# The order of loads at the start of a fused attention and two-layer kernel: one key load to another queue, one weight load earlier, a first weight piece cut smaller

## The chip, the cores and the metric

The kernel runs on one core of one Trainium2 chip. The metric is device time in microseconds (us) of one execution. Where this text gives times inside an execution, they are read from one profiled execution and counted from its first instruction. Engines are named as in the profile: PE is TensorE, DVE is VectorE, ACT is ScalarE, POOL is GpSimd and SP is SyncE.

## The reference

The first half is linear attention with a decay per head, in blocks of 64 positions (4 batches, 8 heads, 768 positions, 64 per head):

```python
for b in range(nb):                       # 12 blocks of 64
    intra = einsum('bhic,bhjc->bhij', qb, kb) * Dmask      # decayed, causal
    intra = einsum('bhij,bhjd->bhid', intra, vb)
    inter = einsum('bhid,bhde->bhie', qb * lam_pow, kv_state)
    out[:, :, sl] = intra + inter
    kv_state = lam_block * kv_state + einsum('bhsd,bhse->bhde', kb * rev_pow, vb)
```

Its output, laid out as 3072 tokens of 512 values, goes through two matrix products with an activation between them:

```python
h = x @ w_in                                       # 512 -> 2048
g = maximum(h, 0) + alpha * minimum(h, 0)          # alpha per column
return g @ w_out                                   # 2048 -> 512
```

Inputs and the output are float32. The kernel multiplies in float16.

## The kernel before

**Tiles.** The 3072 tokens are worked on as six chunks of 512. A chunk `c` holds 256 positions (a window) of two batches; `bi` is 0 or 1 for the batch. For the attention a chunk is four units of work, `units = [(c, bi, hh)]`, where `hh` is one half of the heads. So units 0 to 3 are chunk 0, units 4 to 7 are chunk 1, and units 4 and 5 need the loads of (1,0), units 6 and 7 those of (1,1).

**Loads.** `fetch` (line 77) loads q, k or v of one (c, bi): for the early chunks it is one DMA of 128 partitions by 8 heads by 128 values, and `part` cuts it to half of the heads. `load` (line 99) puts it on SP's queue as float32 (512 KB; 256 KB for a half). `load16` (line 109) puts it on GpSimd's queue, which casts to float16 on the way (256 KB written). GpSimd's queue also carries the weights: `load_win` (line 115) a range of columns of w_in, `load_wout` (line 121) a range of row blocks of w_out (four blocks of 128 rows, 512 KB written, in one DMA). `hold` (line 95) writes one value into a key tile on DVE, so that the tile is claimed there and the load orders itself behind that write.

**Steps of a unit.** `cast(n, x, engine)` turns the float32 keys or queries of unit n to float16; `key_decayed` multiplies keys by the decay into `kdec` on GpSimd; `turn` transposes keys and then queries on PE into one PSUM bank (tag `tk`), and `turned` copies both out, on ACT or DVE; `decayed` scales the turned queries into `qdT`. `cluster(old, new)` issues on PE the scores of the unit `new` and the outputs of the unit `old`, and the products of decayed keys and values for the state. `masked` applies the decay mask on DVE, `state` and `aged` carry the state forward, and `out_of` copies the unit's output into `xT`, the input of the first product.

**Steps of the two products.** `up(c, f, bi, slot)` does four matmuls for 128 columns of `h` into the PSUM bank named by `slot` (for both batches at once when `bi` is None, 512 wide, else 256 wide); `below` takes the negative part on ACT into `m`; `gate` combines both on DVE into `g` and so frees the bank. `down(c, t, part, slot)` adds a quarter of the sum over 2048 for the output tile `t` (four matmuls, row blocks 4·part to 4·part+3 of w_out) in a bank that it holds until `store` copies the tile out on ACT and writes it. `slopes(slot)` transposes alpha on PE and makes `oma`, which `gate` needs, on DVE. `fill` issues matmuls without a use for their result.

**Order.** Tile tracks the data dependences, but the program order on every engine is as the steps are called. For chunks 0 and 1 that is a list of calls written out by hand, lines 787 to 1175. Chunks 2 to 5 are woven by a loop (from line 1255). Each engine works through its own instructions in that order, and an instruction that waits holds everything behind it on its engine, the issue of DMAs included. What matters around the change is this stretch of the list, GpSimd's and SP's loads in it being:

```python
    load_wout(0, 4)         # 879, GpSimd
    load("k", 1, 0)         # 888, SP
    load("k", 1, 1)         # 889, SP
    load16("q", 1, 0)       # 892, GpSimd
    load16("v", 1, 0)       # 924, GpSimd
    load16("q", 1, 1)       # 937, GpSimd
    load16("v", 1, 1)       # 943, GpSimd
    key_decayed(4, "G")     # 944, waits for k(1,0)
    load_wout(4, 4)         # 954, GpSimd
    load_wout(8, 4)         # 957, GpSimd
```

Of the kernel before, what the change touches and what calls it, by code (L numbers as in the profile page):

```python
# [11 lines left out]
def kernel(  # L12
# [16 lines left out]
    nc = tc.nc  # L29
# [47 lines left out]
    def fetch(queue, src, x, c, bi, part):  # L77

        h0, n = (0, H) if part is None else (part * H // 2, H // 2)
        pb, b = c // 2, 2 * (c % 2) + bi  # L80
        x, rows = x[:, ds(h0, n), :], src[b, ds(h0, n), ds(pb * W, W), :]
        if c < FIRST:
            queue.dma_start(out=x, in_=rows.rearrange("h (p e) d -> p h (e d)", e=2))  # L83
        else:
            for e in range(2):
                queue.dma_start(out=x[:, :, ts(e, D)], in_=rows[:, ts(e, L), :].rearrange("h p d -> p h d"))

    def raw(x, c, bi):
        if (c, bi, x) not in raws:
            raws[c, bi, x] = raw_pool.tile(  # L90
                [128, H, 2 * D], fp32, tag=f"{x}raw", name=f"{x}raw", bufs={"k": 5, "q": 4}[x]
            )
        return raws[c, bi, x]
# [2 lines left out]

        nc.vector.memset(raw(x, c, bi)[0:1, part * H // 2, 0:1], 0.0)

    def load(x, c, bi, part=None):
        fetch(nc.sync, {"k": k, "q": q}[x], raw(x, c, bi), c, bi, part)  # L100

    def rows16(x, c, bi):
        if (c, bi, x) not in halves16:
            halves16[c, bi, x] = half_pool.tile(
                [128, H, 2 * D], fp16, tag=f"{x}h", name=f"{x}h", bufs={"q": 4, "v": 6}[x]
            )
        return halves16[c, bi, x]

    def load16(x, c, bi, part=None):
        fetch(nc.gpsimd, {"q": q, "v": v}[x], rows16(x, c, bi), c, bi, part)  # L110
# [4 lines left out]
    def load_win(c0, n):  # L115
        nc.gpsimd.dma_start(  # L116
            out=w_in_sb[:, :, ds(c0, n)],
            in_=moe_w_in[:, ds(c0, n)].rearrange("(g p) f -> p g f", p=128),
        )

    def load_wout(f0, n):
        nc.gpsimd.dma_start(
            out=w_out_sb[:, ds(f0, n), :],
            in_=moe_w_out[ds(f0 * 128, n * 128), :].rearrange("(f p) d -> p f d", p=128),
        )
# [153 lines left out]
    def decay_mask(hp):  # L279
        nc.scalar.activation(  # L280
            dmask[:, :, hp].rearrange("p h e j -> p h (e j)"),
            MK.pop(hp)[:, 0:384].rearrange("p (h x) -> p h x", h=2),
            AF.Exp,
        )
# [9 lines left out]
    def key_decay():  # L294
        nc.scalar.activation(kdecay, klog, AF.Exp)
# [4 lines left out]
    def query_log():  # L300

        x = ps.tile([128, 2, 512], fp32, tag="acc", name="ql_ps")
        QL.append(x[:, 0].rearrange("p (hh e hp j) -> p hh e hp j", hh=2, e=2, hp=2))
        for h in range(H):
            hh, hl, hp = h // 4, h % 4 // 2, h % 2
            nc.tensor.matmul(
                QL[0][ds(hl * 64, 64), hh, :, hp, :],
                lhsT=parts[:, h : h + 1].to_broadcast([128, 64]),
                rhs=col16[:, 128:256].rearrange("p (e j) -> p e j", e=2),
                start=True,  # L310
                stop=True,
            )
# [56 lines left out]
    def bank(slot, name):  # L369
        return ps.tile([128, CH], fp32, tag=slot if slot == "tk" else f"b{slot}", name=name)  # L370

    def slopes(slot):
        at = bank(slot, "at_ps")
        nc.tensor.transpose(at[:, 0:NF], alpha_sb, ident32)
        nc.vector.tensor_scalar(
            out=oma, in0=at[:, 0:NF], scalar1=-1.0, scalar2=1.0, op0=ALU.mult, op1=ALU.add
        )
# [18 lines left out]
    def copy_on(eng, out, in_):  # L396
        if eng == "A":
            nc.scalar.activation(out, in_, AF.Copy)  # L398
        elif eng == "V":
            nc.vector.tensor_copy(out=out, in_=in_)  # L400
        else:
            nc.gpsimd.tensor_copy(out=out, in_=in_)
# [4 lines left out]
    def view(t, hh):  # L407
        return t[:, ds(4 * hh, 4), :].rearrange("p h (e d) -> p e h d", e=2)
# [8 lines left out]
    def cast(n, x, eng):  # L417
        c, bi, hh = units[n]
        t = T.setdefault(n, {})
        if (c, bi) in Q16 and x == "q":  # L420
            out = view(rows16(x, c, bi), hh)
        elif (c, bi) in Q16:
            out = t["k16"] = half_pool.tile([128, 2, 4, D], fp16, tag="k16", name="k16", bufs=4)
        else:
            if "qk16" not in t:
                t["qk16"] = half_pool.tile([128, 2, 2, 4, D], fp16, tag="qk16", name="qk16")
            out = t["qk16"][:, int(x == "k")]
        if (c, bi) in Q16 and x == "q":
            copy_on(eng, out, view(raws[c, bi, x], hh))
        else:  # L430

            copy_on(
                eng,
                out.rearrange("p e s d -> p s e d"),
                raws[c, bi, x][:, ds(4 * hh, 4), :].rearrange("p (hl hp) ed -> p hp hl ed", hp=2),
            )
# [38 lines left out]
    def turned(n, eng):  # L475
        t = T[n]
        if len(eng) == 2:

            for x in (1, 0):
                y = qkt_pool.tile([128, 2, 2, L], fp16, tag=f"{'qk'[x]}T", name=f"{'qk'[x]}T", bufs=1)  # L480
                t["qk"[x] + "T"] = y
                copy_on(eng[1 - x], y, t["tp"][x])
        else:
            y = qkt_pool.tile([128, 2, 2, 2, L], fp16, tag="qkT", name="qkT")
            t["qT"], t["kT"] = y[:, 0], y[:, 1]
            copy_on(eng, y, t["tp"])
# [228 lines left out]
    def up(c, f, bi, slot):  # L715
        n = CH if bi is None else W
        h_ps = HP[c, f, bi] = bank(slot, "h_ps")
        for gi in range(NHP):
            x = XT[c][:, gi]
            nc.tensor.matmul(  # L720
                h_ps[:, 0:n] if bi is None else h_ps[:, 0:n].rearrange("p (e j) -> p e j", e=2),
                lhsT=w_in_sb[:, gi, ts(f, 128)],
                rhs=x.rearrange("p e b j -> p (e b j)") if bi is None else x[:, :, bi, :],
                start=(gi == 0),
                stop=(gi == NHP - 1),
            )

    def below(c, f, bi):
        n = CH if bi is None else W
        m = M[c, f, bi] = m_pool.tile([128, CH], fp32, tag="m", name="m")  # L730
        nc.scalar.activation(m[:, 0:n], HP[c, f, bi][:, 0:n], AF.Relu, scale=-1.0)  # L731

    def gate(c, f, bi):
        n = CH if bi is None else W
        if (c, f) not in G:
            G[c, f] = g_pool.tile([128, 2, 2, L], fp16, tag=f"g{f}", name=f"g{f}")
        g, m, h_ps = G[c, f], M.pop((c, f, bi)), HP.pop((c, f, bi))
        if bi is None:
            g, mv, hv = g.rearrange("p e b j -> p (e b j)"), m, h_ps
        else:  # L740
            g = g[:, :, bi, :]
            mv, hv = (y[:, 0:n].rearrange("p (e j) -> p e j", e=2) for y in (m, h_ps))
        nc.vector.scalar_tensor_tensor(  # L743
            out=g, in0=mv, scalar=oma[:, f : f + 1], in1=hv, op0=ALU.mult, op1=ALU.add
        )

    def down(c, t, part, slot=2, nparts=4):

        if part == 0:
            O[c, t] = bank(slot, "o_ps")  # L750
        n = NF // nparts
        for f in range(part * n, part * n + n):
            nc.tensor.matmul(  # L753
                O[c, t],
                lhsT=G[c, f][:, t // 2, t % 2, :],
                rhs=w_out_sb[:, f, :],
                start=(f == 0),
                stop=(f == NF - 1),
            )
# [55 lines left out]
    small_identity("G")  # L815
    pair_logs()
    mask_log(1)
    slopes(2)
    key_decay()
    turn(0)  # L820
    decay_mask(0)
    cast(1, "k", "V")
    query_log()
    decay_mask(1)
    key_decayed(0, "G")
# [4 lines left out]
    fill(4)  # L830
    decayed(0, "V")
    cluster(None, 0)
    load_win(0, 256)
    mask_log(3)
    cast(1, "q", "A")
    state(0, 0)
    key_decayed(1, "G")
    masked(0, 0)
    masked(0, 1)
    load_win(256, 256)  # L840
    fill(4)
    turn(1, True)
    decay_mask(3)
# [42 lines left out]
    gate(0, 0, 0)  # L886
    hold("k", 1, 0)
    load("k", 1, 0)
    load("k", 1, 1)
    below(0, 1, 0)  # L890
    gate(0, 1, 0)
    load16("q", 1, 0)
# [29 lines left out]
    below(0, 5, None)  # L922
    gate(0, 4, None)
    load16("v", 1, 0)
    gate(0, 5, None)
    up(0, 7, None, 2)
    below(0, 6, None)
# [12 lines left out]
    below(0, 10, None)  # L940
    gate(0, 10, None)
    up(0, 12, None, 1)
    load16("v", 1, 1)
    key_decayed(4, "G")
    key_decayed(5, "G")
# [5 lines left out]
    below(0, 12, None)  # L951
    gate(0, 12, None)
    down(0, 2, 0, 0)
    load_wout(4, 4)
    turn(4)
    up(0, 13, None, 1)
    load_wout(8, 4)
# [58 lines left out]
    cluster(6, 7)  # L1016
    below(1, 1, 0)
    gate(1, 1, 0)
    down(0, 0, 3, 2)
    out_of(6, "A")  # L1020
    masked(7, 0)
    state(7, 0)
    up(1, 2, 0, 1)
    hold("k", 2, 1)
    masked(7, 1)
    aged(7, 1)
# [9 lines left out]
    store(0, 2)  # L1036
    gate(1, 2, 0)
    turn(8)
    cast(9, "k", "V")
    up(1, 4, 0, 1)  # L1040
    below(1, 3, 0)
    load16("v", 3, 0)
    turned(8, "V")
    up(1, 5, 0, 0)
    below(1, 4, 0)
    gate(1, 3, 0)
# [259 lines left out]
```

## Time and profile before

| what | value |
|---|---|
| median of 3 runs | 217.38 us (217.02 to 218.69) |
| profiled execution, whole time | 217.07 us |
| its span, first to last instruction | 215.3 us |
| granted TensorE clock | 1.000 |
| PE busy | 206.1 us, 96% of the span |
| DVE, ACT, POOL busy | 123.0, 112.6, 97.4 us |
| moved by DMA | 28.43 MB |
| GpSimd's queue (q0, software) | 8.65 MB, 26592 packets |
| SP's queue (q1, hardware) | 13.11 MB, 40800 packets |

The page's chain of work that ended last names, at each step back from the last instruction, what released it. A line such as `33.92 0.41 PE L471 MATMUL tp<-ident,qh ... x8 [1.24 <-DMA qh<-in_q_dram]` of the timeline reads: at 33.92 us, for 0.41 us, PE ran eight matmuls of line 471 that write `tp` and read `ident` and `qh`; PE had been idle for 1.24 us before, and what ended that was the DMA into `qh`. `PEld` is the loading of matmul weights, which overlaps with matmuls. A name such as `kraw` stands for all tiles of the kind. In the queue lines, packets, megabytes and the time that the packets took as a share of the stretch on 16 DMA engines are given; packets overlap, so shares can add to over 100%.

### The profile page before, as it was taken

Reading aid. Unit: us, or ns where it says so; the run is one execution under the profiler, and the core shown is the slowest. Engines: PE = TensorE matmul, PEld = TensorE weight load, DVE = VectorE, ACT = ScalarE, POOL = GpSimd, SP = SyncE. Lnnn points to the kernel's source line nnn. Section 1 sums busy time; section 2 is a strip of 40 time slices with the busy share of each in tenths; the row PEclk is TensorE's granted clock in tenths of the full one; section 3 lists DMA queues with packets and bytes.
Section 4 is the critical chain, followed back from the end, with each engine's and each line's share of the span. In section 5 each row is a group of like instructions: output and inputs, shape, how many; then the busy total and the mean of one; then the engine's idle time right before and its main releaser. Section 6 shows DMA issues by size and latency. Waiting matters only on the chain.

```text
span 215.3 us, 5683 instructions
## 1 busy us (share of the span) xinstructions
PE 206.1 (96%) x2350; PEld 106.0 (49%) x2350; DVE 123.0 (57%) x259; ACT 112.6 (52%) x213; POOL 97.4 (45%) x155
## 2 busy tenths in 40 slices
PE   7978997899999999999999999999999999999993
PEld 2656543557665545454444444544444444444442
DVE  2787783849768785456576556756654344443000
ACT  5966665536656565465555555454444434443121
POOL 7899428867889561973895256422000000000000
PEclk9999999999999999999999999999999999999999
DMA  4999999999999494697689995313011101100212
GB/s 116 251 189 181 208 215 190 209 209 207 272 250 252 105 214 35 150 194 100 102 93 216 216 219 112 80 53 97 0 52 50 43 9 49 49 27 24 97 59 89
DMA packets 71194, 28.43 MB, mean 132 GB/s; under 512 B 52080, under 2 KB 68224, under 8 KB 71168
## 3 DMA queue, kind: packets, MB, share of 16 engines
q0 software_dynamic: 26592, 8.65, 35.9%
q1 hardware_dynamic: 40800, 13.11, 32.0%
q10 hardware_dynamic: 3776, 6.31, 8.1%
q8 instruction: 18, 0.29, 0.6%
q14 instruction: 8, 0.07, 0.1%
HBM read 27.28 MB, written 6.29 MB: 156 GB/s over the span
## 4 chain that ended last, share of the span: by engine, by line
PE 80%; DMA 7%; POOL 6%; ACT 3%; issue 1%; DVE 0%; ACTq 0%; POOLq 0%
PE h_ps L720 34%; PE o_ps L753 32%; DMA qh<-in_q_dram 7%; PE o_ps L775 6%; PE acc L552 3%; POOL kdec L444 2%; PE s L600 2%; PE acc L572 2%; POOL w_in_sb L116 2%; PE tp L471 1%; ACT qkT L398 1%; PE tp L466 1%; POOL qdT L508 1%; PE acc L617 1%; ACT L248 1%
## 5 line engine op out<-in xcount | busy, mean ns | idle before, releaser
L743 DVE SCALAR_TENSOR_TENSOR g<-m,oma,h_ps 128x512 f16<-128x512 f32 (+1 forms) x106 | 73.0, 696 | 64.1 <-ACT m L731 62.4
L720 PE MATMUL h_ps<-xT,w_in_sb 128*128 128x512 f16 (+1 forms) x424 | 96.7, 359 | 1.0 <-ACT R L679 0.6
L731 ACT ACTIVATE m<-h_ps 128x512 f32<-128x512 f32 (+1 forms) x106 | 59.0, 556 | 55.8 <-PE h_ps L720 53.9
L753 PE MATMUL o_ps<-w_out_sb,g 128*128 128x512 f16 x320 | 81.2, 379 | 0.0
L720 PEld LDWEIGHTS <-w_in_sb 128*128 128x128 f16 x424 | 39.6, 98 | 41.6 <-DMA w_in_sb<-in_moe_w_in_dram 1.1
L753 PEld LDWEIGHTS <-g 128*128 128x128 f16 x320 | 30.9, 98 | 35.8
L764 ACT ACTIVATE o_sb<-o_ps 128x512 f32<-128x512 f32 (+2 forms) x25 | 14.5, 579 | 18.8 <-PE o_ps L775 11.0
L444 POOL TENSOR_TENSOR kdec<-kraw,kdecay 128x256 f16<-128x256 f32 x32 | 19.5, 633 | 7.4 <-DMA kraw<-in_k_dram 6.6
L633 DVE TENSOR_TENSOR sm<-s,dmask 128x512 f16<-128x512 f32 x32 | 21.2, 684 | 2.8 <-PE s L600 2.7
L398 ACT ACTIVATE xT<-acc 128x512 f16<-128x512 f32 x22 | 13.1, 597 | 13.3 <-PE acc L572 9.0
L508 POOL TENSOR_TENSOR qdT<-qkT,nqdecay 128x512 f16<-128x512 f16 x8 | 9.3, 1164 | 18.9 <-DMA qkT<-qk 8.7
L701 POOL TENSOR_TENSOR old<-R,rdecay 128x128 f32<-128x128 f16 x21 | 8.3, 410 | 17.4 <-DVE R L681 14.8
L775 PE MATMUL o_ps<-w_out_sb,g 128*128 128x512 f16 (+2 forms) x80 | 14.0, 336 | 0.0
L508 POOL TENSOR_TENSOR qdT<-qkT,qdecay 128x512 f16<-128x512 f16 (+1 forms) x11 | 11.3, 1029 | 3.0 <-DVE qkT L400 1.9
L552 PE MATMUL acc<-qdT,R 64*64 64x64 f16 (+1 forms) x216 | 10.9, 217 | 0.2
L775 PEld LDWEIGHTS <-g 128*128 128x128 f16 x80 | 7.2, 98 | 6.9
L685 DVE SCALAR_TENSOR_TENSOR R<-R,nrdecay,s 128x64 f16<-128x64 f16 x48 | 10.5, 275 | 0.0
L552 PEld LDWEIGHTS <-R 64*64 64x64 f16 x224 | 5.9, 104 | 8.8 <-issue 5.9
L444 POOL TENSOR_TENSOR kdec<-kraw,nkdecay 128x256 f16<-128x256 f32 x16 | 9.5, 613 | 0.0
L572 PE MATMUL acc<-sm,vh 64*64 64x128 f16 (+1 forms) x352 | 8.5, 209 | 0.0
L83 POOL DMA_DIRECT2D vh<-in_v_dram x8 | 7.6, 945 | 0.8 <-POOLq L1290 0.8
L398 ACT ACTIVATE qk<-qraw 128x512 f16<-128x512 f32 x11 | 6.9, 624 | 2.0 <-DMA qraw<-in_q_dram 1.1
(107 smaller groups left out, 152.3 us busy)
## 6 DMA issues: line engine op xcount, KB each, us to landing
out_dram<-o_sb ACTq DMA_DIRECT2D x23, 256.0 KB, 2.3
kraw<-in_k_dram SPq DMA_DIRECT2D x12, 256.0 KB, 5.1
kraw<-in_k_dram SPq DMA_DIRECT2D x6, 512.0 KB, 11.4
qraw<-in_q_dram SPq DMA_DIRECT2D x10, 256.0 KB, 6.9
vh<-in_v_dram POOLq DMA_DIRECT2D x8, 256.0 KB, 10.5
w_out_sb<-in_moe_w_out_dram POOLq DMA_DIRECT2D x4, 512.0 KB, 9.4
w_in_sb<-in_moe_w_in_dram POOLq DMA_DIRECT2D x3, 512.0 KB, 6.7
qh<-in_q_dram POOLq DMA_DIRECT2D x5, 256.0 KB, 11.1
```

Of the source, the lines that this page charges most:

```text
L398: nc.scalar.activation(out, in_, AF.Copy)
L444: engine(eng).tensor_tensor(out=kdec[:, e], in0=kr[:, e], in1=decay.unsqueeze(2).to_broadcast([128, 4, D]), op=ALU.mult,)
L508: engine(eng).tensor_tensor(out=out, in0=src, in1=(qdecay if c < FIRST else nqdecay)[:, hh].rearrange("p e h j -> p (e h) j").unsqueeze(2) ...
L552: nc.tensor.matmul(o, lhsT=before[ds(hl * 64, 64), hp, :], rhs=x, start=not own and e == 0, stop=False, skip_group_check=True,)
L572: nc.tensor.matmul(o, lhsT=vo[p, e, hp + 2 * hl, :], rhs=x, start=(2 * pbo + a == 0 and hl == 0 and e == 0), stop=(e == 1 or co >= FIRST), ...
L633: nc.vector.tensor_tensor(out=t["sm"][hl], in0=t["s"][:, hl].rearrange("p (h x j) -> p h x j", h=2, x=2), in1=mask_of(hl, hh), op=ALU.mult,)
L720: nc.tensor.matmul(h_ps[:, 0:n] if bi is None else h_ps[:, 0:n].rearrange("p (e j) -> p e j", e=2), lhsT=w_in_sb[:, gi, ts(f, 128)], rhs=x ...
L731: nc.scalar.activation(m[:, 0:n], HP[c, f, bi][:, 0:n], AF.Relu, scale=-1.0)
L743: nc.vector.scalar_tensor_tensor(out=g, in0=mv, scalar=oma[:, f : f + 1], in1=hv, op0=ALU.mult, op1=ALU.add)
L753: nc.tensor.matmul(O[c, t], lhsT=G[c, f][:, t // 2, t % 2, :], rhs=w_out_sb[:, f, :], start=(f == 0), stop=(f == NF - 1),)
L764: nc.scalar.activation(o_sb[:, 0:n], o_ps[:, 0:n], AF.Copy)
L775: nc.tensor.matmul(o_ps[:, 0:n], lhsT=G[c, f][:, t // 2, t % 2, :], rhs=w_out_sb[:, f, ds(c0, n)], start=(f == 0), stop=(f == NF - 1),)
```

## The change

Six edits, all in the hand-written order, and a parameter for the queue of `load`:

- the load of k for (1,1) is issued on GpSimd's queue, between v(1,0) and q(1,1), where it was issued on SP's queue behind k(1,0);
- the second piece of w_out (row blocks 4 to 7) is issued ahead of v(1,1), where it was issued behind `key_decayed` of units 4 and 5;
- the first two pieces of w_in have 128 and 384 columns, where both had 256;
- `slopes` is called after the second cast of keys, where it was called ahead of the first `turn`;
- `up(1, 2, 0, 1)` is called ahead of `down(0, 0, 3, 2)`, where it was called behind it and three more steps;
- the cast of unit 9's keys is called behind `turned` of unit 8, where it was ahead of it.

```diff
-    def load(x, c, bi, part=None):
-        fetch(nc.sync, {"k": k, "q": q}[x], raw(x, c, bi), c, bi, part)
+    def load(x, c, bi, part=None, queue=nc.sync):
+        fetch(queue, {"k": k, "q": q}[x], raw(x, c, bi), c, bi, part)
...
     mask_log(1)
-    slopes(2)
     key_decay()
     turn(0)
     decay_mask(0)
     cast(1, "k", "V")
+    slopes(2)
     query_log()
...
-    load_win(0, 256)
+    load_win(0, 128)
...
-    load_win(256, 256)
+    load_win(128, 384)
...
     load("k", 1, 0)
-    load("k", 1, 1)
     below(0, 1, 0)
...
     load16("v", 1, 0)
+    load("k", 1, 1, None, nc.gpsimd)
     gate(0, 5, None)
...
     up(0, 12, None, 1)
+    load_wout(4, 4)
     load16("v", 1, 1)
     key_decayed(4, "G")
     key_decayed(5, "G")
...
     down(0, 2, 0, 0)
-    load_wout(4, 4)
     turn(4)
...
     gate(1, 1, 0)
+    up(1, 2, 0, 1)
     down(0, 0, 3, 2)
     out_of(6, "A")
     masked(7, 0)
     state(7, 0)
-    up(1, 2, 0, 1)
     hold("k", 2, 1)
...
     turn(8)
-    cast(9, "k", "V")
     up(1, 4, 0, 1)
     below(1, 3, 0)
     load16("v", 3, 0)
     turned(8, "V")
+    cast(9, "k", "V")
     up(1, 5, 0, 0)
```

## The prediction

> **What bounds the kernel now.** I read the page's head and chain, then busy time by stage, then PE's waits, then the stage where PE waits.
>
> ```profile
> span 215.3 us, 5683 instructions
> PE 206.1 (96%) x2350; PEld 106.0 (49%) x2350; DVE 123.0 (57%) x259; ACT 112.6 (52%) x213; POOL 97.4 (45%) x155
> ...
> PE 80%; DMA 7%; POOL 6%; ACT 3%; issue 1%; DVE 0%; ACTq 0%; POOLq 0%
> ```
> PE sets the time, with one transfer in the chain that ended last. By stage (first two columns: stretch and length; then PE's busy time):
>
> ```profile
> 16.60:32.50 15.90, 15.52 (x152) 8.86 (x152) 12.48 (x24) 10.28 (x22) 9.33 (x15) 1.00 1.25 201
> 32.50:42.40 9.90, 7.91 (x150) 4.51 (x146) 5.71 (x13) 6.05 (x10) 8.29 (x14) 1.00 1.48 198
> 42.40:66.00 23.60, 23.54 (x414) 14.97 (x414) 17.04 (x37) 13.23 (x28) 18.31 (x27) 1.00 1.39 238
> 66.00:211.70 145.70, 145.63 (x1421) 69.55 (x1418) 77.06 (x152) 70.45 (x123) 47.16 (x72) 1.00 0.53 98
> ```
> From 42.4 us PE is idle 0.13 us in all. It is idle 1.99 us between 32.5 and 42.4 and 3.15 us before 16.6; nothing else can be won. A stall removed there is worth its length, as long as no later transfer or bank makes PE wait again. PE's longest wait after the start, and GpSimd's program around it:
>
> ```profile
> PE tp L471 <- DMA qh<-in_q_dram: 1.2, 1, 1.2
> ```
> ```profile
> 33.92 0.41 PE L471 MATMUL tp<-ident,qh 128*64 128x128 f16 x8 [1.24 <-DMA qh<-in_q_dram]
> ```
> ```profile
> 19.14 0.90 POOL L83 DMA_DIRECT2D qh<-in_q_dram  x1
> 20.04 1.49 POOL L701 TENSOR_TENSOR old<-R,rdecay 128x128 f32<-128x128 f16 x4
> 21.46 0.94 POOL L83 DMA_DIRECT2D vh<-in_v_dram  x1
> 22.39 0.89 POOL L83 DMA_DIRECT2D qh<-in_q_dram  x1
> 23.26 0.90 POOL L83 DMA_DIRECT2D vh<-in_v_dram  x1
> 30.71 2.52 POOL L444 TENSOR_TENSOR kdec<-kraw,kdecay 128x256 f16<-128x256 f32 x4 [6.55 <-DMA kraw<-in_k_dram]
> 33.18 1.57 POOL L122 DMA_DIRECT2D w_out_sb<-in_moe_w_out_dram  x2
> ```
> These are q(1,0), v(1,0), q(1,1), v(1,1) of the second chunk. q(1,0) is issued at 19.14 and lands 14.73 us later (chain), at 33.87. Issue time plus time to landing gives the others: w_out's first piece 30.23, k(1,0) 30.55, k(1,1) 34.63, v(1,0) 35.52, q(1,1) 37.03, v(1,1) 38.46, w_out's second, third and fourth pieces 40.96, 43.50, 47.12. They are limited by the queues and not by the issue: DMA is over 90% busy from 5 to 70 us. The DMA view from 30 to 33 us, then from 34.7 to 36.2 (packets, MB, share):
>
> ```profile
> q1 hardware_dynamic: 821, 0.42, 68.7%
> q0 software_dynamic: 823, 0.21, 67.7%
> ```
> ```profile
> q0 software_dynamic: 1073, 0.27, 181.9%
> ```
> While SP's queue (q1) holds k(1,1), it and GpSimd's queue (q0) alternate packet for packet: q0 gets 823 in 3 us, and alone 1073 in 1.5 us. So q(1,0), with PE waiting, is slowed 2.6 times by keys that ACT first casts at 37.30.
>
> **Part by part.**
>
> *k(1,1) from SP to GpSimd, behind v(1,0).* One DMA of 512 KB leaves SP (0.66 us of issue there, free) and joins GpSimd's program at about 0.9 us, the price of q and v. GpSimd has 6.55 us idle ahead of 30.71, so this is free; without that cover it would delay kdec by 0.9. q(1,0) now shares only with k(1,0), until 30.55. Alone, successive q and v land 1.51 and 1.43 us apart. So q(1,0) lands between 30.23 + 1.47 = 31.7 and one more microsecond, 32.7; I take 32.0. PE is free for it at 32.68. **The 1.24 us go.** v(1,0) follows at 33.5 (needed at 36.35 - 1.24 = 35.1).
> The trace has no uncast load on GpSimd's queue. Bounds for its 1024 packets of 512 B: as q's 256 B packets, 1.45 us; as the first piece of w_in, whose 512 packets of 512 B landed 2.42 us after what was ahead (16.36 less 13.94), 4.84 us. Nearest are SP's own packets of 512 B almost alone (978 packets of both queues in the 1.5 us from 7.5: 1.57 us for 1024) and w_in's cast ones (814 packets in 13 to 15 us: 2.5 us). I take 2.0, below the middle, since nothing is cast.
>
> The Trainium skill ("DMA: Bandwidth & Descriptors", "Issuing engine by pattern") gives a simple load to Sync and calls that path generally faster; its fit for GpSimd's path ("Anatomy of one DMA") would make 512 KB 2.0 + 1.2 = 3.2 us, an estimate from that page; k(1,1) would land at 36.7, q(1,1) at 38.2, and PE would move 0.1 and lose 0.23. The trace's 1.43 to 1.51 us between landings of 256 KB disagrees (the fit gives 2.6): back to back the fixed part is not paid again.
>
> *w_out's second piece ahead of v(1,1).* Its issue (0.82 us) moves from 33.18 into the same idle time; the third piece is issued that much earlier, behind the same backlog. Pieces of w_out land 2.50 and 2.54 us apart. New landings with 2.0 for k: k(1,1) 35.5, q(1,1) 37.0, w_out second 39.5, v(1,1) 41.0, third 43.5, fourth about 47.1; each 0.5 earlier to 2.8 later with k's price. What each allows PE to move forward, as its present time of need less the landing:
> - cast of k(1,1), ACT 37.30: 1.8
> - q(1,1), PE 38.31: 1.3
> - w_out second, PE 41.38: 1.9 (behind v(1,1), as now, it would land near 41.0 and allow 0.3)
> - v(1,1), PE 44.25: 3.2
> - w_out third, PE 44.93: 1.4
> All over 1.24, q(1,1) just so.
>
> *up(1,2,0,1) ahead of the fourth quarter of the first output tile.* Four matmuls pass four on PE. They need the bank that gate(1,1,0) empties:
>
> ```profile
> 46.65 0.60 PE L720 MATMUL h_ps<-xT,w_in_sb 128*128 128x256 f16 x4
> ...
> 48.01 1.04 PE L753 MATMUL o_ps<-w_out_sb,g 128*128 128x512 f16 x4
> 48.89 0.60 PE L720 MATMUL h_ps<-xT,w_in_sb 128*128 128x256 f16 x4
> ```
> ```profile
> 47.71 0.48 DVE L743 SCALAR_TENSOR_TENSOR g<-m,oma,h_ps 128x256 f16<-128x256 f32 x1 [1.36 <-ACT m L731]
> ```
> The gate ends at 48.19, the moved matmuls could go at 48.01, and the handover takes some 0.05: **0.23 us lost**, where down's matmuls had covered it. Behind them wait those matmuls, the store of the tile on ACT, and up(1,3), whose bank the store frees: 50.41 against 50.42, no more lost. In return the fourth piece of w_out is needed 0.67 us later.
>
> *cast(9) behind turned(8) on DVE.* The cast takes 0.84; turned(8), at 51.76, can go when its transposes end, near 51.35. cluster(7,8) starts its scores 0.22 us after the matmuls ahead, elsewhere 0.07: gain 0 to 0.15. turn(9), at 53.24, has its keys by 52.9.
>
> *slopes later.* The transpose (0.23) and the DVE step (0.17) now lie behind turn(0); turned(0) starts 0.3 later and ends at 8.67, just when qdecay (ACT, to 8.64) lets the next DVE step go. 0 to 0.1 lost; taken as 0.
>
> *w_in 128 and 384.* Two DMAs as before, the same bytes; the first lands up to 0.7 earlier. PE's first use began at 16.65 with ACT's work ending at 16.60: gain 0 to 0.2, taken as 0. The second use, at 18.00, needs the second piece, still due near 17.3.
>
> **The sum.** -1.24 + 0.23 = -1.0; from 50 us on, k(2,1) lands at 58.33 for a GpSimd cast of 0.61 us ahead of PE's turn at 59.66. If it does not land earlier, it allows 59.66 + 0.23 - 59.04 = 0.85 and the net is -0.6; issued a microsecond earlier it may move too. With that and turned(8) I take -0.9: span 214.4. The profiled execution took 217.07, 1.8 around its span, so 216.2; it lies 0.3 under the median of 217.38, so the forecast is **216.5**.
>
> **Rivals.**
> - *The gain is taken by the next landing* (chance 0.18). DMA is full until 70 us; if q(1,1) lands at 37.9 instead of 37.0, PE moves 0.4 and loses 0.23: 217.2. For it: the small margin there. Against it: unmixed queues move a pair of packets in about 47 ns an engine (22 + 25), mixed in 58, so the total shrinks.
> - *k(1,1) is dear on GpSimd's queue: slower* (0.19). In place: cast of k on ACT and q(1,1) on PE, in turn(6). At 4.84 us k lands at 38.3 and q(1,1) at 39.8, 1.5 past its present use: with 0.23, +1.7, 219.1. It decides from about 3 us on. For it: no such transfer in the trace, and w_in's slow first piece. Against it: the rate of 512 B packets on both queues.
> - *The start moves too* (0.05): 0.2 of w_in, 0.15 of turned(8) and most of the four short gaps of 0.75 us in all between 35 and 40 us add to 1.24: 215.3.
> - *Nothing is freed* (0.04): q(1,0) lands late without k(1,1) beside it; 217.6 with the 0.23.
>
> **How the numbers follow.** The forecast, 216.0 to 217.0, has 0.54. The range, 215.3 to 219.1, reaches from the third rival to the second. One per cent, about what a measurement of this kernel can tell from no change, is 2.2 us. Faster by more needs the third rival and a little more: 0.07. Slower by more needs k dearer than its upper bound, or mishaps beside it: 0.15, since that price is the one thing unseen. Within: 0.78.
>
> **What would show it.** Right: no wait of PE on qh near 32.7, q(1,0) landing by 32.7, PE idle under 1 us from 32.5 to 42.4, a gap of 0.2 ahead of the moved up(1,2), PE dense after. Wrong: a wait of ACT or GpSimd on kraw near 36, of PE on qh at turn(6) over 0.5 us, on w_out at down, or k(1,1) more than 3 us behind v(1,0).

## The result and the profile after

The changed kernel takes 217.00 us (median of 22 runs, 216.08 to 219.03), the kernel before 217.84 us (22 runs, 216.96 to 219.33). The ratio is 0.9959, 95% interval 0.9939 to 0.9979: 0.9 us faster, between 0.5 and 1.3.

The profiled execution of the changed kernel is nevertheless a long one, 218.61 us with a span of 216.8, against 217.07 and 215.3. The head of its page and its chain:

```profile
span 216.8 us, 5686 instructions
PE 206.9 (95%) x2350; PEld 106.5 (49%) x2350; DVE 123.7 (57%) x259; ACT 112.8 (52%) x213; POOL 98.5 (45%) x156
...
PE 81%; DMA 10%; DVE 3%; ACT 3%; issue 1%; ACTq 0%; DVEq 0%; POOLq 0%
PE h_ps L720 34%; PE o_ps L753 31%; PE o_ps L775 6%; DMA kraw<-in_k_dram 6%; DMA vh<-in_v_dram 4%; PE acc L552 2%; PE s L600 2%; PE acc L572 2%; DVE g L743 1%; PE tp L471 1%; ACT m L731 1%; PE tp L466 1%; DVE qdT L508 1%; PE acc L617 1%; ACT o_sb L764 1%
```
The transfer of q(1,0) has left the chain, and one into `kraw` has taken its place. The extra length is at the start: the first `up` begins at 18.50 us instead of 16.65. The very first loads landed late: the second half of the first keys at 8.82 us instead of 7.06, and the first values at 10.96 instead of 9.00. DVE waited for the keys, then PE for the values, and it is from the landing of the values that this profile's chain runs on to the first `up`:

```profile
8.84 0.75 DVE L400 CAST qk<-kraw 128x512 f16<-128x512 f32 x1 [2.00 <-DMA kraw<-in_k_dram]
```
```profile
11.10 0.32 PE L617 MATMUL acc<-vh,kdec 64*64 64x64 f16 x16 [0.36 <-DMA vh<-in_v_dram]
```
Nothing in the change stands ahead of these two loads. In the twelve experiments' profiles the first `up` starts at 16.49 to 17.38 us, the changed kernel run again (below) among them at 17.27, so this was a draw of that execution. To compare profiles I therefore count from the first `up` to the end of PE's last matmul: 195.07 us before, 194.71 after. In this stretch the profile's list of PE's waits shows what replaced the wait for qh:

```profile
PE h_ps L720 <- DVE g L743: 1.3, 4, 0.5
```
The timeline of PE at those places, and of ACT and DVE at the first of them:

```profile
34.85 0.41 PE L471 MATMUL tp<-ident,qh 128*64 128x128 f16 x8
35.78 1.02 PE L720 MATMUL h_ps<-xT,w_in_sb 128*128 128x512 f16 x4 [0.52 <-DVE g L743]
...
38.28 1.02 PE L720 MATMUL h_ps<-xT,w_in_sb 128*128 128x512 f16 x4 [0.43 <-DVE g L743]
...
49.44 0.60 PE L720 MATMUL h_ps<-xT,w_in_sb 128*128 128x256 f16 x4 [0.16 <-DVE g L743]
...
52.94 1.03 PE L720 MATMUL h_ps<-xT,w_in_sb 128*128 128x256 f16 x8 [0.17 <-DVE g L743]
```
```profile
33.84 0.63 ACT L398 ACTIVATE k<-kraw 128x512 f16<-128x512 f32 x1 [1.39 <-DMA kraw<-in_k_dram]
34.37 0.58 ACT L731 ACTIVATE m<-h_ps 128x512 f32<-128x512 f32 x1
```
```profile
34.98 0.75 DVE L743 SCALAR_TENSOR_TENSOR g<-m,oma,h_ps 128x512 f16<-128x512 f32 x1 [0.72 <-ACT m L731]
```
The queries of turn(4) run with no wait: the 1.24 us are gone. But in this execution k(1,0) landed at 33.81 us, 15.3 after the first `up` (13.9 before). ACT's cast waits for it for 1.39 us, and `below`, queued behind the cast, is late; so are the gate behind it and the bank for the next `up`: 0.52, and the same once more one bank on, 0.43. The last two waits are those of the moved up(1,2,0,1) and of the second `up` behind it.

GpSimd's program of loads is as the change has it, and its issues end 6.21 us before k(1,0), which its next step needs, has landed:

```profile
23.42 0.94 POOL L83 DMA_DIRECT2D vh<-in_v_dram  x1
24.36 0.90 POOL L83 DMA_DIRECT2D kraw<-in_k_dram  x1
25.24 0.89 POOL L83 DMA_DIRECT2D qh<-in_q_dram  x1
26.11 0.77 POOL L122 DMA_DIRECT2D w_out_sb<-in_moe_w_out_dram  x1
26.86 0.91 POOL L83 DMA_DIRECT2D vh<-in_v_dram  x1
33.98 0.76 POOL L444 TENSOR_TENSOR kdec<-kraw,kdecay 128x256 f16<-128x256 f32 x1 [6.21 <-DMA kraw<-in_k_dram]
```
They land, in the order of the queue: v(1,0) 35.52, k(1,1) 37.39, q(1,1) 38.43, w_out's second piece 40.96, v(1,1) 42.41, its third 45.02, fourth 48.69. From v(1,0) to k(1,1) it is 37.39 - 35.52 = 1.87 us. The load behind gains some of it back: q(1,1) lands 1.04 after k(1,1), where it landed 1.51 after v(1,0) before, so k(1,1) holds up what is queued behind it by 1.40.

### The profile page after: what moved, and what is told of

Same layout as the page of the kernel before. It is cut to its first block, busy times and chain, and to the rows that moved or that the text cites. A ratio compares the mean times of both kernels' runs of the same rounds, so it can differ in the third digit from the quotient of the medians.

```text
span 216.8 us, 5686 instructions
## 1 busy us (share of the span) xinstructions
PE 206.9 (95%) x2350; PEld 106.5 (49%) x2350; DVE 123.7 (57%) x259; ACT 112.8 (52%) x213; POOL 98.5 (45%) x156
## 4 chain that ended last, share of the span: by engine, by line
PE 81%; DMA 10%; DVE 3%; ACT 3%; issue 1%; ACTq 0%; DVEq 0%; POOLq 0%
PE h_ps L720 34%; PE o_ps L753 31%; PE o_ps L775 6%; DMA kraw<-in_k_dram 6%; DMA vh<-in_v_dram 4%; PE acc L552 2%; PE s L600 2%; PE acc L572 2%; DVE g L743 1%; PE tp L471 1%; ACT m L731 1%; PE tp L466 1%; DVE qdT L508 1%; PE acc L617 1%; ACT o_sb L764 1%
## 5 line engine op out<-in xcount | busy, mean ns | idle before, releaser
L764 ACT ACTIVATE o_sb<-o_ps 128x512 f32<-128x512 f32 (+2 forms) x25 | 14.5, 579 | 19.4 <-PE o_ps L775 11.0
L384 PE MATMUL op_fill<-filler 128*128 128x512 f16 x17 | 6.8, 541 | 2.7 <-DVE sel L203 1.1
```

The lines of the kernel that those rows point to most:

```text
L764: nc.scalar.activation(o_sb[:, 0:n], o_ps[:, 0:n], AF.Copy)
```

## Experiments

Ratios are to runs of the kernel before on the same chip. "Stretch" is from the first `up` to PE's end in the one profiled execution; gaps are PE's of 0.15 us or more, behind the first `up`. Left out, but for the rows of before and after, are the short ones around the turns of units 5 to 7 (0.12 to 0.29 each), which nearly every kernel has.

| kernel | ratio (95%) | stretch | gaps of PE and what ended them |
|---|---|---|---|
| before | 1 | 195.07 | 1.24 qh, then 0.15, 0.12, 0.19 and 0.29 around the turns |
| changed | 0.9959 (0.9939 to 0.9979) | 194.71 | above |
| changed, again | 0.9982 (0.9961 to 1.0003) | 194.72 | 0.16 and 0.17 gates, 0.26 k(2,1) |
| k(1,1) moved alone | 0.9987 (0.9954 to 1.0019) | 195.85 | 0.83 w_out, 0.25 outputs of unit 11, 0.66 scores |
| changed, k(1,1) back | 0.9987 (0.9967 to 1.0008) | 195.29 | 0.55 qh, 0.16 and 0.17 gates, 0.29 scores |
| changed, up(1,2) back | 0.9955 (0.9923 to 0.9986) | 194.41 | 0.43 k(2,1) |
| start edits alone | 1.0007 (0.998 to 1.0034) | 195.80 | 1.40 qh, 0.20 w_out |
| k(1,1) and w_out moved | 0.9962 (0.994 to 0.9983) | 194.83 | 0.52 and 0.43 gates, 0.17 w_out, 0.43 scores |
| changed, w_out back | 0.9975 (0.9945 to 1.0006) | 194.37 | 0.16 w_out, 0.16 and 0.17 gates |
| k(1,1) late on SP | 1.0084 (1.0057 to 1.0111) | 197.91 | 2.92 cast of k(1,1), 0.16 and 0.17 gates |
| k(1,1) in halves | 0.9942 (0.9907 to 0.9977) | 194.14 | 0.16 and 0.17 gates |
| changed, start back | 0.9979 (0.9961 to 0.9998) | 194.05 | 0.16 and 0.16 gates |
| halves, up(1,2) back | 0.997 (0.9949 to 0.9991) | 194.76 | 0.19 gate, 0.31 w_out, 0.36 scores |
| halves, k(1,0) early | 0.9945 (0.993 to 0.996) | 194.54 | 0.23 w_out, 0.16 and 0.16 gates |

**1. The move of k(1,1) alone.** On the kernel before:

```diff
     load("k", 1, 0)
-    load("k", 1, 1)
...
     load16("v", 1, 0)
+    load("k", 1, 1, None, nc.gpsimd)
```


> Kernel before with one edit: k(1,1) issued on GpSimd's queue between v(1,0) and q(1,1). Theory (the gain is the wait for q(1,0), worth about 1.2 us, and the later weight piece has to follow or it takes most of it back): PE's wait for qh ahead of turn(4) is gone, but the second piece of w_out, unmoved, lands about 41 us on the clock of the profile before and lets PE move 0.3 to 0.5 us only; 217.3 to 217.6 against 217.84 before, ratio 0.997 to 1.000, with a wait of PE at down(0,0,1). Rival (all of the gain is in this one edit): ratio 0.995, no wait at down. Second rival (the gain is in the start, not here): ratio 1.000, no change in PE's idle time from the first up() on.

The wait for qh is gone, and the median is not told apart from before. So far the theory holds; the place does not. The second piece landed in time, at 40.51. It was the fourth that PE waited for, at down(0,0,3):

```profile
48.08 1.02 PE L753 MATMUL o_ps<-w_out_sb,g 128*128 128x512 f16 x4 [0.83 <-DMA w_out_sb<-in_moe_w_out_dram]
```
It was issued at 38.2 and landed at 48.04. The rest went at 72 to 73 us, in `cluster(11, 12)`: the outputs of unit 11 waited 0.25 for DVE's state, and the scores of unit 12 0.66 for the tile that is turned by DMA.

**2. k(1,1) back on SP, all else changed.** Undoing that edit:

```diff
     load("k", 1, 0)
+    load("k", 1, 1)
...
-    load("k", 1, 1, None, nc.gpsimd)
```


> Changed kernel with k(1,1) back on SP's queue behind k(1,0); all other edits stay. Theory: q(1,0) shares its packets with k(1,1) again, PE waits for it by 1 us or more, and the moved up(1,2) costs its 0.16 to 0.23; ratio to before 1.000 to 1.002. Rival (the gain comes from the other edits): ratio 0.996, as the changed kernel.

The wait for qh is back. The interval of the ratio takes in the theory's 1.000 and not the rival's 0.996, but it overlaps with that of the changed kernel (from 0.9967 to 0.9979). The wait is 0.55 and not 1 us, because this execution's first `up` came 0.7 us later while the queue did not. The interval leaves up to 0.3% for the other edits.

**3. up(1,2,0,1) back.**

```diff
-    up(1, 2, 0, 1)
     down(0, 0, 3, 2)
     out_of(6, "A")
     masked(7, 0)
     state(7, 0)
+    up(1, 2, 0, 1)
```


> Changed kernel with up(1,2,0,1) behind state(7,0) again. Theory (the move costs 0.16 to 0.23 us for nothing as long as w_out's fourth piece lands in time): the gap ahead of the moved matmuls is gone, 0.1 to 0.2 us faster than the changed kernel, ratio to before 0.994 to 0.996. Rival (the move pays, because the fourth piece of w_out would be waited for): a wait of PE at down(0,0,3) on w_out_sb and ratio 0.996 to 0.998.

Both gate gaps are gone, and w_out's fourth piece landed at 46.88, in time. The medians, 216.69 here and 217.00 for the changed kernel, lie too close for their intervals. New is a wait of 0.43 at turn(11) for GpSimd's cast of k(2,1).

**4. The two edits of the start alone**, on the kernel before:

```diff
-    slopes(2)
...
     cast(1, "k", "V")
+    slopes(2)
...
-    load_win(0, 256)
+    load_win(0, 128)
...
-    load_win(256, 256)
+    load_win(128, 384)
```


> Kernel before with the two edits of the start: slopes behind the second cast of keys, w_in's first pieces 128 and 384 columns. Theory: no effect, ratio 0.999 to 1.001, and whether PE's first up() starts near 16.6 or near 18.5 us is decided by when the first keys land, in either kernel. Rival (the late start in the profile of the changed kernel, 18.50 against 16.65, is the work of slopes): first up() near 18.5 and ratio 1.005 or more. Second rival (the start edits bring part of the gain): ratio 0.998 or less.

No effect that these runs can tell, and the first `up` at 16.90. The wait for qh is there in full, which shows it a second time without the other edits.

**5. k(1,1) and w_out's second piece.** Experiment 1 and, in addition:

```diff
+    load_wout(4, 4)
     load16("v", 1, 1)
...
     down(0, 2, 0, 0)
-    load_wout(4, 4)
```


> Kernel before with two edits: k(1,1) on GpSimd's queue behind v(1,0), and w_out's second piece ahead of v(1,1). up(1,2,0,1), slopes, w_in and the cast of unit 9 stay. Theory (these two carry the whole gain): no wait for qh, no wait for w_out over 0.2 us; 0.8 to 1.1 us faster, ratio 0.995 to 0.997. Rival (the moved up(1,2) is needed too): PE waits 0.4 us or more for w_out's fourth piece at down(0,0,3), as in the run with k(1,1) alone (0.83 us), ratio 0.998 to 1.000.

The ratio, 0.9962, is that of the changed kernel: these two edits give the gain, as far as these runs can tell. In its profile k(1,0) again landed late, 15.2 us behind the first `up`, with the same pair of gaps, 0.52 and 0.43, as in the changed kernel's. So these do not come from the other edits either.

**6. w_out's second piece back, all else changed.**

```diff
-    load_wout(4, 4)
     load16("v", 1, 1)
...
     down(0, 2, 0, 0)
+    load_wout(4, 4)
```


> Changed kernel with w_out's second piece behind the keys' decay again; k(1,1) stays on GpSimd's queue and up(1,2,0,1) stays moved. Theory of the prediction (that piece has to go ahead of v(1,1) or PE waits for it at down(0,0,1)): it lands within 0.3 us of its use, a wait of 0 to 0.5 us there, ratio 0.996 to 0.998. Rival (the second piece is not the one that binds: with k(1,1) alone it landed in time, and the fourth piece, issued 0.8 us later, is late): no wait at down(0,0,1), the fourth piece is covered by the moved up(1,2) up to 0.4 us; ratio 0.996 or less.

```profile
40.42 0.81 PE L753 MATMUL o_ps<-w_out_sb,g 128*128 128x512 f16 x3 [0.16 <-DMA w_out_sb<-in_moe_w_out_dram]
```
It lands at 40.38, right at its use: the order is worth 0.16 us here. That is within the theory's 0 to 0.5 us; the rival had no wait there. The ratio, 0.9975 with an interval from 0.9945 to 1.0006, fits both.

**7. Order or queue: k(1,1) late on SP.**

```diff
-    load("k", 1, 1, None, nc.gpsimd)
...
     gate(0, 8, None)
+    hold("k", 1, 1)
+    load("k", 1, 1)
```


> Changed kernel, with k(1,1) back on SP's queue, but issued late: a second write of one value into its tile on DVE behind gate(0,8) holds it until about 28 us. All other edits stay. Theory (what counts is that its packets don't run beside those of q(1,0), whichever queue carries them): first packets about 3.5 us behind the issue, so behind most of q(1,0); q(1,0) lands by 33, wait for qh under 0.3 us, k(1,1) lands at 35 to 37; ratio 0.995 to 0.998. Rival (GpSimd's queue itself is the cheaper carrier, and beside it SP's packets of 512 B slow v(1,0) and q(1,1)): q(1,1) lands 1 us or more later than in the changed kernel, PE waits in turn(6), ratio 0.998 to 1.001.

Half of the theory holds: q(1,0) landed at 32.74 and PE did not wait for it, so its packets had only to be kept free of those of k(1,1). The other half fails, and so does the rival: the load was issued at 29.13, its first packets ran near 33, and they then shared one for one with q(1,1) and w_out's second piece. It landed some 10 us after its issue, not at 35 to 37, while q(1,1) was only 0.5 us later than in the changed kernel. The waits of PE and of ACT:

```profile
PE tp L466 <- ACT k L398: 2.9, 1, 2.9
```
```profile
ACT k L398 <- DMA kraw<-in_k_dram: 2.6, 1, 2.6
```
At 1.0084 this is the slowest kernel of the study. A place in GpSimd's queue, taken at 24 us, is a place in the order; a late issue on another queue is not. An issue on SP some microseconds earlier, whose first packets would have come right behind q(1,0), was not tried, so it is not shown that the order could not be had with SP's queue too.

**8. The price of a DMA in that queue: two halves.**

```diff
-    load("k", 1, 1, None, nc.gpsimd)
+    load("k", 1, 1, 0, nc.gpsimd)
+    load("k", 1, 1, 1, nc.gpsimd)
```


> Changed kernel with k(1,1) loaded on GpSimd's queue as two DMAs of 256 KB, the halves of the heads. Theory (back to back in the queue only the bytes and packets cost): from the landing of v(1,0) to that of the second half 1.7 to 2.3 us (1.87 for the whole in the changed kernel), GpSimd 0.7 to 0.9 us more of issue in its idle time, ratio as the changed kernel, 0.995 to 0.997. Rival (each DMA on this queue pays a fixed 2 us, the rule of the Trainium skill, DMA: Bandwidth & Descriptors): 3.5 us or more between those landings, PE waits 1 us or more for q(1,1), ratio 1.000 or more.

v(1,0) lands at 33.13, the halves at 34.03 and 34.98: 0.90 and 0.95, together 1.85, the same as the whole. The second DMA added nothing that shows. The Trainium skill ("DMA: Bandwidth & Descriptors", "Anatomy of one DMA") has a fixed cost of about 2.0 us for each DMA. These landings, 0.90 and 0.95 us apart, do not show it paid again by a DMA that stands behind others in a full queue.

**9. The changed kernel again.** No edit.

> The changed kernel once more, as it is, to have it on the same chip as the three kernels below. Theory (the start and the landing of k(1,0) vary from execution to execution; the late first up() at 18.50 and the two gaps of 0.52 and 0.43 us behind turn(4) in its profile are such a draw): ratio 0.994 to 0.998, first up() between 16.5 and 17.5 us this time, and no wait of ACT for kraw over 0.6 us if k(1,0) lands within 14.5 us of the first up(). Rival (both belong to the change): first up() near 18.5 and the same two gaps again.

First `up` at 17.27, k(1,0) 14.5 us behind it, no pair of gaps: the same kernel gives both, so both are draws of the execution. Experiment 4 bears this out for k(1,0), which landed 15.3 us behind the first `up` with the old order of loads too. The ratio, 0.9982, is less good than the first one; their intervals overlap from 0.9961 to 0.9979. This one alone does not exclude that nothing was gained.

**10. The start undone in the changed kernel**: the diff of experiment 4, backwards.

> Changed kernel with the two edits of the start undone: slopes ahead of the first turn, w_in's first pieces 256 and 256. Theory (they do nothing): ratio to before equal to the changed kernel's within 0.002; w_in's first piece lands near 16.4 us, where it landed near 14.7 with 128 columns, and the first up() still starts between 16.5 and 17.4. Rival (the smaller piece lets the first up() start sooner): first up() 0.2 us or more later than with it, ratio 0.001 higher.

No effect: 0.9979 beside 0.9982. w_in's first piece lands at 16.53 here with 256 columns and at 14.6 to 15.1 in nine of the ten profiles with 128, and the first `up` does not begin sooner for it.

**11. Halves, up(1,2) back:** the edits of 8 and 3 together.

> Changed kernel with k(1,1) as two halves on GpSimd's queue and up(1,2,0,1) behind state(7,0) again. Theory (the moved up(1,2) costs 0.16 and, later, 0.17 us; with the store no longer pushed back neither gap is there): the gaps 30.2 and 33.7 us behind the first up() are gone; 0.1 to 0.4 us faster than the changed kernel, ratio 0.993 to 0.996. Rival (it pays as cover for w_out's fourth piece): a wait of PE on w_out_sb of 0.2 us or more at down(0,0,3), ratio as the changed kernel or higher.

The rival this time: the two gate gaps are gone, and w_out's fourth piece, landing at 47.33, is waited for by 0.31. With experiments 1, 3 and 5 this makes waits of 0.83, 0, 0.17 and 0.31 for that piece where up(1,2) is not moved and the wait for qh is gone, against a steady 0.33 where it is. The move neither pays nor costs anything that these runs can tell.

**12. Halves, and k(1,0) issued earlier.**

```diff
+    hold("k", 1, 0)
+    load("k", 1, 0)
     up(0, 0, 0, 2)
...
     gate(0, 0, 0)
-    hold("k", 1, 0)
-    load("k", 1, 0)
```


> Changed kernel with k(1,1) as two halves on GpSimd's queue and k(1,0) held and issued on SP's queue ahead of the first up() instead of behind the first gate, some 2.5 us earlier. Theory (k(1,0) is what binds turn(4) now in some executions): it lands 1 us or more earlier against the first up(), no gap of 0.4 us or more behind turn(4); but w_out's first piece shares packets with it sooner and may land 0.2 to 0.4 later, a wait of PE at down(0,0,0) of up to 0.4 us; ratio 0.992 to 0.996. Rival (nothing left to win there): ratio as the changed kernel, or 0.998 and more if w_out's first piece is late.

k(1,0) lands 9.4 us behind the first `up`, over 4 us earlier than anywhere else, and the pair of gaps has no cause left. The price came as expected:

```profile
PE o_ps L753 <- DMA w_out_sb<-in_moe_w_out_dram: 0.2, 1, 0.2
```
Its median of 216.16 us is the lowest measured, over five runs that span 0.6 us. Its interval (0.993 to 0.996) lies just below that of the changed kernel on the same chip (0.9961 to 1.0003); which of its two edits does it was not taken apart, and its one profile does not show where: the stretch, 194.54, is longer than that of the halves alone, 194.14.

## Why the prediction was right

The forecast was 216.5 us, 0.9 below the median of then; measured are 0.84 between the medians and 0.9 by the ratio, and 0.5 between the medians when the kernel was run again. The mechanism was the one forecast. That the number fits this well is in part luck, since later waits take back more or less of the gain from one execution to the next. In its two profiles the changed kernel's stretch is 0.36 and 0.35 shorter than the one of before. In experiments 8 and 10, where neither k(1,0) nor k(2,1) made PE wait, it is 0.93 and 1.02 shorter. By its steps:

- **The wait for qh.** Right: 1.24 us gone in each kernel with k(1,1) behind v(1,0), 0.55 and 1.40 in the two without. q(1,0) lands 15.5 to 16.2 us behind the first `up` in the kernels with the changed order, where 32.0 us meant 15.4 and the bounds were 15.1 and 16.1: later than taken, and hardly ahead of its use. In the changed kernel run again, at 16.17, PE waited 0.07 for it, and in experiment 5, at 16.16, it came 0.04 ahead.
- **The price of k(1,1) on GpSimd's queue.** 2.0 taken, 1.87 measured, 1.83 to 1.88 in the others with one DMA for it: the size is right, and the rival that it is dear is out. The basis was not right: the price was taken between bounds for 1024 packets of 512 bytes, and the load went as 128 of 4096 (below), so that the two agree is luck. The landings behind it, counted from the first `up`, were given as 18.9, 20.4, 22.9, 24.4 and 26.9, and came at 18.9, 19.9, 22.5, 23.9 and 26.5; those behind k(1,1) came 0.4 us earlier than given, as it held them up by 1.40 only.
- **w_out's second piece.** The direction is right, the size was not: unmoved it was to allow 0.3 us of shift, which would have left a wait of 0.9; PE waited 0.16, since the piece landed 23.7 us behind the first `up` and not at the 24.4 that 41.0 us meant. The piece that took the gain back was the fourth. By the prediction's own figures it allowed 0.9 without the move of up(1,2), as it was to land at 47.1 and was needed at 48.01; it was left out of the list of margins, and only said to be needed 0.67 later.
- **up(1,2).** 0.23 forecast, 0.16 measured. "No more lost" was wrong: up(1,4) waits another 0.17 for the next gate. In the sum this is 0.33 for 0.23.
- **cast(9) behind turned(8).** In the changed kernel's timeline the scores of cluster(7,8) follow the matmuls ahead by 0.01 us instead of 0.22: which looks like the upper end of the 0 to 0.15. But experiments 4 and 5, which leave this cast where it was, show the same 0.01, and experiment 1 shows 0.10. So the 0.22 was seen in the one execution of before alone, and no run shows a gain from this edit. The place in experiment 4:

```profile
53.40 0.24 PE L552 MATMUL acc<-qdT,R 64*64 64x128 f16 x2
53.41 0.46 PE L600 MATMUL s<-qkT 64*64 64x128 f16 x16
```
- **The start.** Taken as nothing, and nothing: 1.0007, and 0.9979 beside 0.9982.
- **The next landing.** This rival, given 0.18, is partly true: the shift is capped at turn(11) by k(2,1) (0.43 and 0.26, where the prediction had placed it), at the scores of unit 12 by tiles turned by DMA (0.29 to 0.66 in four kernels, where it had seen no cap), and, not foreseen, by k(1,0) in executions in which that lands over 15 us behind the first `up`. The prediction gave each load behind the move a margin, and k(1,0), which stayed ahead of it, none. By its own sign, PE idle under 1 us from 32.5 to 42.4, the changed kernel's profile fails (1.36), and the kernel run again passes (0.88 in the 10 us from 33). These caps differ from execution to execution, and with them the gain.

## What to carry to other kernels

While DMA is full, a load's place in a queue decides when it lands: give one queue the order in which the tiles are needed, and keep off the other what is not needed yet, since two queues alternate packet for packet (821 and 823 in 3 us before the change) whatever is urgent. When such a wait is taken out, look for the next landing at every later use, those of unmoved loads included: here k(1,0), w_out's second and fourth pieces, k(2,1) and the tiles turned by DMA each made PE wait in some run. Where a profile's start is a draw, compare from an event behind it.

## What the runs showed of the hardware

- The uncast load travels in larger packets on GpSimd's queue. Queue lines of before, then of after:

```profile
q0 software_dynamic: 26592, 8.65, 35.9%
q1 hardware_dynamic: 40800, 13.11, 32.0%
```
```profile
q0 software_dynamic: 26736, 9.18, 36.6%
q1 hardware_dynamic: 39760, 12.59, 32.2%
```
The same 0.52 MB are 1040 packets fewer on SP's queue and only 144 more on GpSimd's: 128 of 4096 bytes, as the trace has them, and 16 small ones. The bounds of the prediction had assumed 1024 of 512 bytes on either. The Trainium skill ("DMA: Bandwidth & Descriptors", "SWDGE vs HWDGE vs iDMA") gives packets of preferably up to 4096 bytes on this path. The trace agrees: 4096 for this load, and 128 to 1024 for the casting ones.
- In experiment 7, with GpSimd's queue deep in backlog, the load issued on SP's queue at 29.13 us sent its first packets at 33.1, some 4 us later, though the load ahead of it had sent its last at 30.4. It landed 10 us after its issue.
- The landing of the first loads varies: the second half of the first keys at 7.0 to 7.6 us in thirteen profiles and 8.8 in one, the first values at 8.95 to 9.74 us and, in that one, at 10.96. There the first `up` began 1.1 us later than in any other.
